# Two-layer attention and MLP step, forward and backward: a turn of w1, eight gradient products, small copies and the last output products change places

## The chip, the core and the metric

The kernel runs on one core of a Trainium2 chip. The metric is the device time of one execution in microseconds. The engines are PE (TensorE, matrix products; PEld are its weight loads), DVE (VectorE), ACT (ScalarE), POOL (GpSimd) and SP (SyncE, which here only issues loads). All loads are issued by SP, in one order; nearly all stores are issued by POOL.

## The reference

One decode step for two sequences (B = 2, one token each, width D = 1024) through attention A, MLP B, attention A, MLP B, with the same weights in both layers, and then the gradients of everything with respect to x, the caches and the weights.

```python
def _A_ref(x, k_cache, v_cache, wq, wo):          # 32 heads, 4 kv heads, 16384 cached keys, head size 128
    q = (x @ wq).reshape(B, Sq, Hq, Dh).transpose(0, 2, 1, 3)
    scores = einsum("bhqd,bhkd->bhqk", q, repeat(k_cache, 8)) * Dh ** -0.5
    o = einsum("bhqk,bhkd->bhqd", softmax(scores), repeat(v_cache, 8))
    return o.transpose(0, 2, 1, 3).reshape(B, Sq, Hq * Dh) @ wo

def _B_ref(x, w1, b1, w2, b2):                    # F = 3584
    h = gelu(einsum("bsd,df->bsf", layernorm(x), w1) + b1)
    return einsum("bsf,fd->bsd", h, w2) + b2

x = x + _A_ref(layernorm(x), ...)                 # layer 0
x = x + _B_ref(layernorm(x), ...)
x = x + _A_ref(layernorm(x), ...)                 # layer 1
x = x + _B_ref(layernorm(x), ...)
out, vjp = jax.vjp(f, x, k_cache, v_cache, wq, wo, w1, b1, w2, b2)
return (out, *vjp(grad_out))
```

Each cache has 2 x 4 x 16384 x 128 bf16 elements, 33.6 MB; its gradient is as large. The outputs are out_0 (x after both layers), out_1 (gradient of x), out_2 and out_3 (gradients of the K and V caches), out_4 to out_9 (gradients of wq, wo, w1, b1, w2, b2).

## The kernel before

**Passes.** The caches are read once for each of four passes: attention forward of layer 0 and of layer 1, then attention backward of layer 1 and of layer 0. A pass runs over 8 positions (one sequence and kv head each) of 16 steps; a step takes 8 rows of 128 keys. In a backward pass (`attn_bwd`) a step turns a block of V on DVE (L537), PE forms scores from it (L550), and 14 steps later K's products (`direct`, L575) collect the gradient of q in columns 0 to 7 of the PSUM tile sb0. At the end of a position `dq_of` copies these columns out, scaled (L1052), and sets them to zero (L1054). In the last pass (layer 0) the cache gradients are formed as well: `kv_outputs` turns blocks of probabilities and slopes (L1233) and multiplies them with the rows of q and of the output gradient (L1252); eight such products fill a 1 MB stage, which POOL stores (L1257).

**The order.** `Program.emit` collects pieces in a list, and `run` lays them out in this order, so that every engine's queue follows the list. Loads are handed out in the order of first use as slots come free (16 slots of 1 MB and some borrowed places). The order around the steps is written by hand: events at a step, background pieces (`bg`, released by a credit that rises with every step), `wb` for the weight products.

**The turn into the last pass.** At the end of the layer 1 backward pass the list is: `tail` (the last products with wq, L465), then the layer norm's backward (`attn_in_bwd`: `sums`, `rest`), which gives the gradient gA1 and its bf16 copy gM_all. Then w2 is multiplied with gM_all (`here_products`, L465, 28 times 8 products), which gives dh (L1504); dh is spread over quadrants (L506, L507) and multiplied with w1 (`turned_products`, L487, list `p1`, 8 times 28 products). For that, w1's eight loads of 896 KB are turned by DVE (`turn_rows`, L437, two turns for each load, list `t1`): two within the pass, two right after it, five among w2's products, seven after dh. The result is put back in order by `unquad` (L517 copies it out of PSUM; 16 small copies L525, L527, L529 on DVE, ACT and POOL go by the letters of `on`), and the MLP's layer norm backward (`mlp_in_bwd`, L649 on) gives gA_all (L929), which the first products of the last pass need (L465 again, with wo).

**Gradient products.** The gradients of the weights are outer products: `y_rows` (L1270) and `x_rows` (L1290) build rows, `dw_units` makes one product of 128 x 512 after the other (L1307), and ACT or DVE copies each out of PSUM (`cast_out`, L276, L279; the engine with the smaller estimated load takes it). Four of them fill a 512 KB stage, which POOL stores (L1333). `first` is the list for out_8 (w2): its first nine pieces stand between w1's products, six more between the MLP norm's two halves; `rest_h`, what is left of it, opens the background list.

**The end.** After the last step `attn_bwd` emits `todo`: the events, K's last output products (`kv_units`), `rows`, `tail`, the gradient products of wq's last part (`units`, 16 of them), and `parts`: the norm's sums (with the sum over partitions on PE, L594), its rest, and the row of out_1 (`col_to_row`, L617, L618, L619).

Of the kernel before, what the change touches and what calls it, by code (L numbers as in the profile page):

```python
# [29 lines left out]
N_END = 133  # L30
# [27 lines left out]
class Program:  # L58
# [12 lines left out]
    def emit(self, fn, uses=()):  # L71
        i = len(self.ops)
        self.ops.append((fn, tuple(uses)))
        for c in uses:
            if c.first is None:
                c.first = i
            c.last = i
# [105 lines left out]
def kernel(  # L183
# [25 lines left out]
    V = nc.vector  # L209
# [5 lines left out]
    _, HKV, SK, DH = A_k_cache.shape  # L215
# [3 lines left out]
    R = HQ // HKV  # L219
# [10 lines left out]
    emit = P.emit  # L230
# [14 lines left out]
    sb = [psp.tile([128, 512], F32, name=f"sb{i}") for i in range(2)]  # L245

    def flat(t):
        return t.rearrange("p a b -> p (a b)")

    half = {(i, f): flat(scb[i][f][:]) for i in range(2) for f in range(2)}  # L250
# [31 lines left out]
    def dve(us):  # L282
        load_of("dve", us)
# [65 lines left out]
    dq_all = vec.tile([128, HQ, 4], BF16, name="dq_all")  # L349
# [9 lines left out]
    saved = {}  # L359
# [150 lines left out]

        return (lambda: hold["vb"]), fn

    def unquad(dst, src, on="vag"):

        C = src.shape[1]
        q = small.tile([128, 8, 4, 2], F32, name="uq", bufs=1)[:, 0:C]
        V.tensor_copy(out=q, in_=src)  # L517
        n = 0
        for a in range(4):
            for j in range(4):  # L520
                d, s_ = dst[32 * a:32 * a + 32, :, j], q[32 * j:32 * j + 32, :, a]
                e = on[n % len(on)]
                n += 1
                if e == "v":
                    V.tensor_copy(out=d, in_=s_)  # L525
                elif e == "a":
                    S.copy(out=d, in_=s_)  # L527
                else:
                    GP.tensor_copy(out=d, in_=s_)  # L529
# [40 lines left out]
    def direct(acc, c, i, x, fresh=True):  # L570

        xv = x[:].rearrange("p (c j h y) -> p c j h y", c=NCH, j=4, y=8)
        for t in range(8):
            n = (i % 4) * 8 + t
            PE.matmul(acc, lhsT=c.ap[:, n * 128:(n + 1) * 128], rhs=xv[:, i // 4, t // 2, :, 2 * (i % 4) + t % 2],  # L575
                      start=(fresh and i == 0 and t == 0), stop=(i == 15 and t == 7),
                      skip_group_check=not fresh)
# [14 lines left out]
    def part_sum(src, n, at=None):  # L592
        ps = (ob() if at is None else at)[:, 0:n]
        PE.matmul(ps, lhsT=onesf, rhs=src, start=True, stop=True)  # L594
        return ps
# [48 lines left out]
        V.tensor_tensor(out=y[:], in0=xc[:], in1=bcast_j(rstd[:], DJ), op=ALU.mult)  # L644
        return y, rstd

    def ln_bwd_sums(dy, y, at=None):
        t1 = wrk.tile([128, DJ, 2], F32, name="lb_t1")
        V.tensor_tensor(out=t1[:], in0=dy, in1=y, op=ALU.mult)  # L649
        s = small.tile([128, 2, 2], F32, name="lb_s")  # L650
        V.tensor_reduce(out=s[:, 0, :], in_=dy.rearrange("p j b -> p b j"), axis=AX.X, op=ALU.add)
        V.tensor_reduce(out=s[:, 1, :], in_=t1[:].rearrange("p j b -> p b j"), axis=AX.X, op=ALU.add)
        return part_sum(flat(s[:]), 4, at)

    def ln_bwd_rest(ps, dy, y, rstd, twice=False):
        nm = small.tile([128, 2, 2], F32, name="lb_nm")
# [280 lines left out]
    vec_y, vec_r = {}, {}  # L937
# [83 lines left out]
                               lambda r: dq_all[:, k * R + r, 2 * l:2 * l + 2], l == 0) for j in range(DJ)]  # L1021
        return turns, prods

    def attn_bwd(l, order, gT, wo_first, outputs=None, mark=None, extra=None):

        kvs = []
        for g in order:
# [6 lines left out]
        ev, wb = {}, {}  # L1034
# [14 lines left out]

        def dq_of(pos, g):  # L1050
            def fn():
                V.tensor_scalar(out=dq_all[:, (g % HKV) * R:(g % HKV + 1) * R, 2 * l + g // HKV], in0=sb[0][:, 0:8],  # L1052
                                scalar1=QSCALE, scalar2=None, op0=ALU.mult)
                V.memset(sb[0][:, 0:8], 0.0)  # L1054
                dve(0.3)
            return fn

        xt = {}
# [8 lines left out]
        for pos, g in enumerate(order):  # L1067
            quick = l == 0 and pos == G - 1
            for f in range(2):
                n = 117 + 5 * f if quick else 16 * pos + 10 + 8 * f  # L1070
# [9 lines left out]
        tail = []  # L1080
        for i, k in enumerate(kvs):
# [16 lines left out]
            else:  # L1098
                if l == 0:
                    wb.setdefault(32 * i + 12 + LAG_B, []).append((dn_kept, ()))  # L1100
                ops, tail = wq_last_ops(l, k)
# [10 lines left out]
        s = 0  # L1112
        while s <= n_steps:
            if s in (10, 74) and mark is not None:
                mark(s // 64)
            pre = list(ev.pop(s, ()))
            fill = list(outputs(s)) if outputs is not None else []
            mids = []
            for v in k_at.get(s, ()):
                vpos, vi = divmod(v, 16)  # L1120
                vg = order[vpos]
                if vi % 4 == 0:
                    vc[0] = ld_kv("K", vg, vi // 4)
                c = vc[0]

                def pk(vpos=vpos, vg=vg, vi=vi, c=c):
                    direct(sb[0][:, 0:8], c, vi, xt[vpos % 2], False)

                mids.append((pk, [c]))
            n = -(-len(fill) // 3)  # L1130
            for fn, us in pre:
                emit(fn, us)
            between = fill[:n] + mids + fill[n:2 * n]
            for v in v_at.get(s, ()):
                pos, i = divmod(v, 16)
                if i % 4 == 0:
                    kc[0] = ld_kv("V", order[pos], i // 4)
                kblock(kc[0], i, scb[0], order[pos], between)
                between = []
            for fn, us in between:  # L1140
                emit(fn, us)
            if s not in v_at and pend:
                emit(*pend.pop(0))
            for fn, us in wb.pop(s, []) + (extra or {}).pop(s, []) + fill[2 * n:]:
                emit(fn, us)
            if l == 0 and s == 122:
                emit(lambda: obanks.extend([half[0, 0], half[0, 1]]))
            s += 1
        aflush()
        parts = attn_in_bwd(l, gT, dnq)  # L1150
        if l == 1:
            todo = tail + parts
        else:
            rows, kv_units, units = outputs(s, True)
            todo = ev.pop(s) + kv_units[0:2] + rows + tail[0:4] + kv_units[2:4] + tail[4:] + units[0:2] + parts[0:1]
            todo += units[2:5] + parts[1:2] + units[5:9] + parts[2:] + kv_units[4:] + units[9:]
        for b in todo:
            emit(*b)
        assert not ev and not wb and not pend and not extra, (ev, wb, extra)
# [1 line left out]
    def attn_in_bwd(l, gT, dnq):  # L1161
        h = {}

        def sums():
            dn = wrk.tile([128, DJ, 2], F32, name="dn")
            last = sb[0][:, 112:128].rearrange("p (j b) -> p j b", b=2)
            if l == 1:
                V.tensor_copy(out=dn[:], in_=last)
            else:
                V.tensor_tensor(out=dn[:], in0=last, in1=dnq[:], op=ALU.add)  # L1170
            h["dn"] = dn
            h["ps"] = ln_bwd_sums(dn[:], vec_y[f"a{l}"][:], half[0, 0] if l == 1 else sb[0][:, 200:])
            dve(0.8)

        def rest():
            dx = ln_bwd_rest(h["ps"], h["dn"][:], vec_y[f"a{l}"][:], vec_r[f"a{l}"][:])
            gn = saved[f"gA{l}"]
            V.tensor_tensor(out=gn[:], in0=dx[:], in1=gT()[:], op=ALU.add)
            dve(1.3)
            if l == 1:  # L1180
                V.tensor_copy(out=gM_all[:, :, 0:2], in_=gn[:])

        res = [(sums, ()), (rest, ())]
        if l == 0:
            res.append(col_to_row(saved["gA0"], out_1.rearrange("b s d -> (b s) d"), nc.sync))
        return res


    def kv_outputs(pos, g):

        res = []
# [28 lines left out]
        for c, w in [(c, w) for c in range(NCH) for w in (1, 0)]:  # L1220
            at_ = base + 4 * c + 4 * (pos == 0) if w == 1 else base + 14 + 4 * c
            if w == 0 and pos == G - 1:
                at_ = (124, 127, N_END + 1, N_END + 3)[c]
            stg = P.chunk(kind="full")
            hold = {}

# [17 lines left out]
                    dve(0.4)  # L1244
                hold["blk"] = blk

            res.append((at_ - 2, turn, ()))
            for u in range(8):
                def unit(c=c, w=w, u=u, hold=hold, stg=stg):
                    ps = ob()  # L1250
# [125 lines left out]
    up = [b * HKV + k for k in range(HKV) for b in range(2)]  # L1376
# [3 lines left out]
    def mark(name):  # L1380
        def f(n=0):
            marks[name, n] = len(P.ops)
        return f
# [56 lines left out]
    ws_o, wo_turns1, wo_prods = wo_first_ops(1, up[0] % HKV)  # L1440
# [27 lines left out]
    extra = {2: [(lambda: V.memset(fps1, 0.0), ())]}  # L1468
# [18 lines left out]
    for n, b in enumerate(t1[0:2]):  # L1487
        extra.setdefault(135 + 2 * n, []).append(b)
    extra[30] = [col_to_row(xM1, out_0.rearrange("b s d -> (b s) d"), kind="load")]
    attn_bwd(1, up, lambda: saved["g3"], (None, wo_prods), mark=mark("d1"), extra=extra)  # L1490
    wo_prods0 = wo_first_ops(0, down[0] % HKV, saved["wo"])[2]


    g2 = saved["gA1"]
    for b in t1[2:4]:
        emit(*b)
    for j in range(FJ):
        emit(*here_products(ws2c[j // 4], (j % 4) * 1024, 8, lambda j=j: dhps0[:, j, :],
# [14 lines left out]
        emit(*b)  # L1513
    emit(lambda: load_of("dve", 6.0))
    first = [y_rows(gM_all, 0, 8, 0, 0)] + dw_units("h", 0, 0, pieces_rows(out_8, F, D))
    rest_h = first[15:]
    for n, b in enumerate(p1):
        emit(*b)
        for u in first[n + (n > 0):n + 2]:
            emit(*u)  # L1520
    va0, spread_a0 = spread(lambda: gA_all[:, :, 0:2], DJ, "va")
    g1p = mlp_in_bwd(0, lambda dm: unquad(dm[:].rearrange("p (c j) b -> p c j b", j=4), dm_0), g2, parts=True)
    emit(g1p[0])
    emit(lambda: load_of("dve", 6.0))
    for u in first[9:15]:
        emit(*u)
    emit(lambda: saved.__setitem__("g1", g1p[1]()))
    extra = {4: [(spread_a0, ())]}
# [91 lines left out]
```

## Time and profile before

| | |
|---|---|
| median of 3 runs | 1110.19 us (1109.47 to 1112.6) |
| the profiled execution | 1110.15 us; span of its instructions 1108.4 us |
| PE, DVE, ACT, POOL busy | 815.9, 761.3, 493.1, 182.6 us |
| DMA | 450.03 MB, mean 406 GB/s |
| mean granted PE clock | 0.82 |
| last pass | about 671 to 1100 us |

The span runs from the first to the last instruction; busy times are sums over an engine's instructions, and the idle time of an engine counts only where others wait for it. In rows of stages the columns are: stretch, its length, busy time and count of each engine, the clock granted to PE, the DMA's busy share and its rate. In rows in order of time: start, length, engine, line, operation, tiles and shapes, and in brackets the idle time before it with what ended it.

### The profile page before, as it was taken

How to read it: one execution, taken by the hardware profiler on the slowest of the kernel's cores; microseconds unless marked ns; L12 is line 12 of the kernel's file. 1: busy time of each engine (PE TensorE's matmuls, PEld its weight loads, DVE VectorE, ACT ScalarE, POOL GpSimd, SP SyncE). 2: the span in 40 equal slices, each digit the busy share in tenths (PEclk: the TensorE clock that was granted, in tenths of full speed). 3: DMA queues.
4: the chain of work that ended last, by engine and by line, in shares of the span. 5: the costliest groups of instructions: out<-in, count | busy, mean ns of one | idle time of the engine just before them, and what ended most of it. 6: DMA issues, size and time to landing. Idle time of an engine off the chain costs nothing. (4 is left out here: it accounts for less than half of the span.)

```text
span 1108.4 us, 34192 instructions
## 1 busy us (share of the span) xinstructions
PE 815.9 (74%) x14689; PEld 609.3 (55%) x14689; DVE 761.3 (69%) x1474; ACT 493.1 (44%) x1133; POOL 182.6 (16%) x577
## 2 busy tenths in 40 slices
PE   5665666456888647888778678878876896698895
PEld 4554555455777547777677564444443443344453
DVE  5864665169888627665546476979776895598984
ACT  0322222102233222235434326767665785487874
POOL 1000000001000000111111101423332332233431
PEclk9999999997555555569868657999897998699998
DMA  9999999999999998999999989999999999999996
GB/s 372 421 422 421 422 425 421 398 404 399 418 423 421 422 421 345 409 419 421 419 423 416 417 318 411 355 399 422 420 420 425 423 419 422 420 402 421 410 423 250
DMA packets 97448, 450.03 MB, mean 406 GB/s; under 512 B 7528, under 2 KB 11638, under 8 KB 58512
## 3 DMA queue, kind: packets, MB, share of 16 engines
q1 hardware_dynamic: 79504, 349.22, 77.3%
q0 software_dynamic: 17792, 98.62, 21.6%
q8 instruction: 115, 1.88, 0.6%
q14 instruction: 37, 0.30, 0.1%
HBM read 349.20 MB, written 98.62 MB: 404 GB/s over the span
## 5 line engine op out<-in xcount | busy, mean ns | idle before, releaser
L537 DVE STREAM_TRANSPOSE kT<-slot 128x512 int32<-128x512 int32 x420 | 283.1, 694 | 112.8 <-PE sc L550 90.2
L550 PE MATMUL sc<-qbd,kT 128*128 128x32 bf16 x4096 | 262.5, 222 | 12.6 <-DVE kT L537 11.0
L550 PEld LDWEIGHTS <-kT 128*128 128x128 bf16 x4096 | 209.1, 115 | 64.7 <-issue 32.9
L575 PEld LDWEIGHTS <-slot 128*128 128x128 bf16 x3520 | 143.9, 103 | 106.7 <-issue 47.1
L575 PE MATMUL sb<-xt,slot 128*128 128x8 bf16 x3520 | 161.1, 176 | 49.0 <-DMA slot<-in_A_v_cache_dram 22.9
L276 ACT CAST slot<-sc 128x512 bf16<-128x512 f32 x293 | 167.0, 592 | 60.4 <-PE sc L1307 38.0
L1252 PE MATMUL sc<-slot,late 128*128 128x512 bf16 x350 | 131.1, 397 | 17.7 <-DVE slot L279 5.7
L279 DVE CAST slot<-sc 128x512 bf16<-128x512 f32 x171 | 114.3, 677 | 27.5 <-PE sc L1252 14.2
L760 ACT ACTIVATE e<-sc 128x512 bf16<-128x512 f32 x32 | 19.0, 597 | 235.9 <-DVE sc L757 169.0
L276 ACT CAST slot<-sb 128x512 bf16<-128x512 f32 x139 | 82.4, 593 | 37.1 <-PE sb L1307 17.0
L455 ACT COPY slot<-tp 128x512 int32<-128x512 int32 x88 | 50.3, 587 | 103.7 <-PE tp L452 103.4
L452 PE MATMUL tp<-ident,slot 128*128 128x128 bf16 x768 | 71.3, 255 | 13.2 <-ACT slot L455 6.0
L1252 PEld LDWEIGHTS <-late 128*128 128x128 bf16 x512 | 44.7, 98 | 62.2 <-issue 48.7
L585 ACT COPY xt<-e 32x128 int32<-32x128 int32 x256 | 75.6, 295 | 3.9
L1252 PE MATMUL sb<-slot,late 128*128 128x512 bf16 x162 | 65.6, 405 | 12.6 <-DVE slot L279 7.7
L1307 PE MATMUL sc<-slot,late 128*128 128x512 bf16 x159 | 64.0, 424 | 11.3 <-DVE e L279 6.2
L437 DVE STREAM_TRANSPOSE slot<-slot 128x1024 int32<-128x1024 int32 (+1 forms) x48 | 55.2, 1176 | 17.0 <-DMA slot<-in_A_wo_dram 8.0
L452 PEld LDWEIGHTS <-slot 128*128 128x128 bf16 x768 | 58.0, 116 | 15.9 <-issue 6.8
L279 DVE CAST slot<-sb 128x512 bf16<-128x512 f32 x81 | 54.9, 678 | 9.7 <-PE sb L1307 4.3
L642 POOL TENSOR_TENSOR m_rstd<-ln_vpe,neghalf 128x2 f32<-128x2 f32 x2 | 1.4, 715 | 349.6 <-DVE ln_vpe L640 349.6
L585 POOL COPY xt<-late 32x64 int32<-32x64 int32 x240 | 55.2, 230 | 13.0 <-DVE late L1046 1.9
L585 POOL COPY xt<-ds 32x64 int32<-32x64 int32 x128 | 29.5, 231 | 159.6 <-DVE ds L1046 104.7
(303 smaller groups left out, 1104.4 us busy)
## 6 DMA issues: line engine op xcount, KB each, us to landing
slot<-in_A_k_cache_dram SPq DMA_DIRECT2D x105, 1024.0 KB, 17.3
slot<-in_A_v_cache_dram SPq DMA_DIRECT2D x98, 1024.0 KB, 17.9
out_dram<-slot POOLq DMA_DIRECT2D x57, 1024.0 KB, 14.6
slot<-in_A_wq_dram SPq DMA_DIRECT2D x25, 1024.0 KB, 16.7
slot<-in_A_wo_dram SPq DMA_DIRECT2D x25, 1024.0 KB, 19.7
out_dram<-slot POOLq DMA_DIRECT2D x43, 512.0 KB, 13.9
slot<-in_B_w_dram SPq DMA_DIRECT2D x23, 896.0 KB, 15.4
slot<-in_B_w_dram SPq DMA_DIRECT2D x12, 1024.0 KB, 13.2
```

The lines of the kernel that those rows point to most:

```text
L276: S.copy(out=dst, in_=src)
L279: V.tensor_copy(out=dst, in_=src)
L437: V.transpose(out=t.ap[:, h * nw * 256:(h + 1) * nw * 256].bitcast(I32).rearrange("p (w j m) -> p w j m", j=4, m=32), in_=c.ap[:, 0:4 * nc ...
L452: PE.transpose(tp[:, j * 128:(j + 1) * 128], c.ap[:, off + j * 128:off + (j + 1) * 128], ident[:])
L455: S.copy(out=d.bitcast(I32), in_=tp.bitcast(I32))
L537: V.transpose(out=kT[:].bitcast(I32).rearrange("p (w j m) -> p w j m", w=4, j=4), in_=c.ap[:, (i % 4) * 1024:(i % 4 + 1) * 1024].bitcast(I ...
L550: PE.matmul(sc[:, a0:a0 + 4, :, 2 * (i % 4) + q], lhsT=kv[:, 2 * q + w, :, e], rhs=qbd[:, q_at(g), 2 * w + e], start=(w == 0 and e == 0), ...
L575: PE.matmul(acc, lhsT=c.ap[:, n * 128:(n + 1) * 128], rhs=xv[:, i // 4, t // 2, :, 2 * (i % 4) + t % 2], start=(fresh and i == 0 and t == ...
L585: (GP.tensor_copy if on[t % len(on)] == "g" else S.copy)(out=d[32 * t:32 * t + 32, c0:c0 + cn, j, :], in_=s[32 * j:32 * j + 32, c0:c0 + cn ...
L760: S.activation(out=e_of(l, g)[:, 8 * f:8 * f + 8].rearrange("p a h b -> p h a b"), in_=sc[f][:].rearrange("p h (a b) -> p h a b", b=8), fu ...
L1252: PE.matmul(ps, lhsT=hold["blk"][:, j, :], rhs=flat(qm(w)[:, (u % 2) * 4:(u % 2) * 4 + 4, :]), start=True, stop=True)
L1307: PE.matmul(ps, lhsT=hold[j // 4 * 4][:, j % 4, :], rhs=Y.ap[:, y_at + c0:y_at + c0 + cn], start=True, stop=True)
```

## The change

Six edits. (1) `unquad` shares its 16 copies by "vgvagvvg" instead of "vag". (2) At the end of the layer 1 pass the third turn of w1 (`t1[2]`) stands between `tail` and the norm instead of behind the norm. (3) In w1's phase only a `y_rows` and an `x_rows` stand between the products, four gradient products follow the sums, and `rest_h` begins at the seventh piece of `first`. (4) The K products of odd positions collect in columns 8 to 15 of sb0. (5) The norm's sums are split: what DVE does, and the sum over partitions on PE as a part of its own (`close`). (6) At the end K's last turn comes before the last step's products, and `todo` is put in another order. The order of loads on SP is the same in both kernels.

```diff
-    def unquad(dst, src, on="vag"):
+    def unquad(dst, src, on="vgvagvvg"):
...
-    def ln_bwd_sums(dy, y, at=None):
+    def ln_bwd_terms(dy, y):
...
-        return part_sum(flat(s[:]), 4, at)
+        return flat(s[:])
+
+    def ln_bwd_sums(dy, y, at=None):
+        return part_sum(ln_bwd_terms(dy, y), 4, at)
...
-    def attn_bwd(l, order, gT, wo_first, outputs=None, mark=None, extra=None):
+    def attn_bwd(l, order, gT, wo_first, outputs=None, mark=None, extra=None, mid=()):
...
-                V.tensor_scalar(out=dq_all[...], in0=sb[0][:, 0:8],
+                acc = sb[0][:, pos % 2 * 8:pos % 2 * 8 + 8]
+                V.tensor_scalar(out=dq_all[...], in0=acc,
                                 scalar1=QSCALE, scalar2=None, op0=ALU.mult)
-                V.memset(sb[0][:, 0:8], 0.0)
+                V.memset(acc, 0.0)
...
-                    direct(sb[0][:, 0:8], c, vi, xt[vpos % 2], False)
+                    direct(sb[0][:, vpos % 2 * 8:vpos % 2 * 8 + 8], c, vi, xt[vpos % 2], False)
...
         if l == 1:
-            todo = tail + parts
+            todo = tail + list(mid) + parts
         else:
             rows, kv_units, units = outputs(s, True)
-            todo = ev.pop(s) + kv_units[0:2] + rows + tail[0:4] + kv_units[2:4] + tail[4:] + units[0:2] + parts[0:1]
-            todo += units[2:5] + parts[1:2] + units[5:9] + parts[2:] + kv_units[4:] + units[9:]
+            todo = ev.pop(s) + kv_units[0:4] + rows + kv_units[4:6] + tail[0:4] + kv_units[6:8] + tail[4:] + kv_units[8:10]
+            todo += parts[0:1] + units[0:4] + parts[1:2] + units[4:8] + parts[2:3] + kv_units[10:13] + parts[3:]
+            todo += kv_units[13:] + units[8:]
...
-            h["ps"] = ln_bwd_sums(dn[:], vec_y[f"a{l}"][:], half[0, 0] if l == 1 else sb[0][:, 200:])
+            h["s"] = ln_bwd_terms(dn[:], vec_y[f"a{l}"][:])
             dve(0.8)
+
+        def close():
+            h["ps"] = part_sum(h["s"], 4, half[0, 0] if l == 1 else sb[0][:, 200:])
...
-        res = [(sums, ()), (rest, ())]
+        res = [(sums, ()), (close, ()), (rest, ())]
...
-                at_ = (124, 127, N_END + 1, N_END + 3)[c]
+                at_ = (124, 127, N_END + 1, N_END + 2)[c]
...
-            res.append((at_ - 2, turn, ()))
+            res.append((min(at_ - 2, N_END - 1), turn, ()))
...
-    attn_bwd(1, up, lambda: saved["g3"], (None, wo_prods), mark=mark("d1"), extra=extra)
+    attn_bwd(1, up, lambda: saved["g3"], (None, wo_prods), mark=mark("d1"), extra=extra, mid=t1[2:3])
...
-    for b in t1[2:4]:
+    for b in t1[3:4]:
         emit(*b)
...
-    rest_h = first[15:]
+    rest_h = first[6:]
     for n, b in enumerate(p1):
         emit(*b)
-        for u in first[n + (n > 0):n + 2]:
-            emit(*u)
+        if n in (3, 5):
+            emit(*first[n // 4])
...
-    for u in first[9:15]:
+    for u in first[2:6]:
         emit(*u)
```

More of the change, by code (lines that the diff above doesn't have):

```diff
@@ L1051, in fn @@
             def fn():
-                V.tensor_scalar(out=dq_all[:, (g % HKV) * R:(g % HKV + 1) * R, 2 * l + g // HKV], in0=sb[0][:, 0:8],
+                acc = sb[0][:, pos % 2 * 8:pos % 2 * 8 + 8]
+                V.tensor_scalar(out=dq_all[:, (g % HKV) * R:(g % HKV + 1) * R, 2 * l + g // HKV], in0=acc,
                                 scalar1=QSCALE, scalar2=None, op0=ALU.mult)
-                V.memset(sb[0][:, 0:8], 0.0)
+                V.memset(acc, 0.0)
                 dve(0.3)
```

## The prediction

> **What bounds the kernel now.** I read the page's DMA rows first: 450 MB at a mean of 406 GB/s, with most slices near 421. At 421 GB/s the bytes alone take 1069 us of the 1108.4 us span. So a change can win only where the DMA stands still or thin, unless it lets an engine catch up that is last. The busy time by stage shows where that is (after the engines come clock, DMA share and GB/s).
>
> ```profile
> 646.00:660.00 14.00, 11.41 (x335) 10.42 (x335) 13.46 (x15) 3.79 (x5) 0.00 (x0) 0.50 0.93 346
> 660.00:664.00 4.00, 4.00 (x111) 3.17 (x109) 2.25 (x3) 2.24 (x4) 0.81 (x2) 0.50 0.25 59
> 692.00:726.00 34.00, 30.30 (x346) 16.07 (x346) 30.95 (x50) 25.96 (x49) 13.51 (x43) 1.00 0.94 350
> 726.00:913.00 187.00, 154.37 (x1806) 81.06 (x1806) 151.01 (x263) 132.63 (x263) 61.33 (x183) 0.93 1.02 421
> 945.00:1086.00 141.00, 120.05 (x1498) 66.82 (x1498) 114.80 (x198) 102.98 (x207) 49.70 (x145) 0.93 1.01 415
> 1086.00:1092.00 6.00, 4.94 (x34) 2.13 (x31) 3.51 (x14) 3.56 (x7) 0.72 (x1) 0.72 0.21 85
> ```
>
> The turn (646 to 664) and the end (1086 to 1092) are thin. From 692 to 726 PE and DVE are about 90% busy and the rate is 350: the engines pace the start of the last pass, and no engine's wait there is on a DMA. From 726 the DMA is full. The chain of waits has one long piece on a load, and none after it:
>
> ```profile
> 913.34 31.38 DMA e<-in_A_v_cache_dram
> ```
>
> So loads pace the pass up to 945; after it engine work is last, with the DMA as full. Next the turn's instructions in order of time (start, length):
>
> ```profile
> 646.00 7.22 DVE L437 STREAM_TRANSPOSE slot<-slot 128x896 int32<-128x896 int32 x7
> 653.15 0.18 DVE L1504 SCALAR_TENSOR_TENSOR dh_all<-sb,nslope 128x56 bf16<-128x56 f32 x1
> 654.77 7.52 DVE L437 STREAM_TRANSPOSE slot<-slot 128x896 int32<-128x896 int32 x7
> 662.32 0.80 SPq L373 DMA_DIRECT2D slot<-in_A_v_cache_dram  x2
> 665.38 0.17 DVE L517 COPY uq<-sb 128x16 f32<-128x16 f32 x1 [3.09 <-PE sb L487]
> 667.53 0.17 DVE L649 TENSOR_TENSOR lb_t<-dm_sb,m_y 128x16 f32<-128x16 f32 x1 [0.90 <-ACT dm_sb L527]
> 670.04 0.17 DVE L929 CAST gA_all<-gM 128x16 bf16<-128x16 f32 x1
> 671.03 1.12 PE L465 MATMUL sb<-gA_all,slot 128*128 128x2 bf16 x36
> ```
>
> **The change, part by part** (against the profiled run: 1108.4 us span, 1110.15 us, 0.04 below the median, so I use its times as they are).
>
> One turn ahead of the norm. The seven turns from 646.00 end at 653.2; PE's products for the same step end at 652.24, so the turns hold L1504 back by 0.9. With six (6 x 1.03) they end at 652.2 and L1504 starts at 652.3: 0.85 saved. The moved turn stands in front of the norm's first copy, L1168 at 643.39, and waits for w1's second load; the landings in the trace put that at 642.34, after the K load whose landing PE waits for at 640.06. 642.34 + 1.03 = 643.37: covered with 0.02 to spare; if the load lands x later, the norm, w2's products behind it and the rest of the turn are x later. I take 0.05. The V load at 662.32 is released by the last turn, so it gains only these 0.85.
>
> Gradient products out of w1's phase. Six of them and three row builds stand between w1's products (L487) and make PE wait for casts; L517 comes at 665.38. Without them L507 ends at 654.0; 224 products at 0.03 each are 6.6, y_rows 0.94, x_rows 0.34: PE ends at 661.9, the seven later turns end at 661.45 and 28 products (0.93) behind them at 662.4. So L517 starts at 662.4: 2.95 earlier, the 0.85 included.
>
> Copies shared otherwise. 16 small copies: DVE 6, ACT 5, POOL 5 become 8, 2, 6. Here ACT's started late behind casts, so L649 came 2.15 after L517. Afterwards DVE needs 8 x 0.173 = 1.39 and POOL 6 x 0.219 = 1.31: 1.63 after L517, 0.5 saved. At 438 ACT was not late, and L649 goes from 1.44 to 1.65 after L517: 0.2 lost, under loads that follow; I take 0. In the three other uses DVE's L994 waits for POOL, whose one more copy costs 0.2; two are before 945 under a full DMA, the third (L994 at 961.61, after waiting 2.48) counts: +0.2.
>
> ```profile
> 438.46 1.06 DVE L525 COPY dm_sb<-uq 32x4 f32<-32x4 f32 x6
> 438.56 1.09 POOL L529 COPY dm_sb<-uq 32x4 f32<-32x4 f32 x5 [22.60 <-DVE uq L517]
> ```
>
> These two run side by side, and POOL's 0.218 each is what dnq's sixteen copies take with nothing beside them (3.51/16). The Trainium skill ("SBUF — State Buffer", SBUF: two separate sides) says that a fp32 copy on VectorE and a GpSimd operation lock each other out for whole instructions; by it the shares would add up, not overlap. The rows do not show that; it is the fourth rival.
>
> Six gradient products behind the sums were on PE until L465 at 671.03, though gA_all was there at 670.2; four are done in time: 0.8 saved. Sum of the turn: 2.95 + 0.5 + 0.8 = 4.25, so the last pass's first products start near 666.8.
>
> What that costs later. In the order of the changed kernel 8 products, one row build and two 512 KB stores go into the background of the last pass, spread over some 115 steps of about 3.1 us. One product writes 131 KB and takes a cast of about 0.635 us on DVE or ACT, half of that with both at work. Up to 726 about 1.6 of them come (0.5 us). From 726 to 945 the DMA is full: 6.4 are still owed at 726 and 2.2 at 945, so 0.55 MB more must pass, 1.3 us at 421 GB/s. After 945 the last 2.2 cost 0.7 by either measure. Sum 2.5; its bounds are 0 (hidden in the engines' waits for loads, about 19 us between 740 and 945) and 5 (8 casts on one engine that is last). I take 2.5, because at a full DMA there is no free place for bytes.
>
> dq in two halves. The accumulator alternates between columns 0 to 7 and 8 to 15 of sb0, so the K products (L575) should no longer wait for the memset (L1054). That wait is 1.6 us in all, 1.1 of it at 1076.30. But both halves lie in one PSUM tile, and in the order of the changed kernel L575 still waits for DVE's memset at each position. I take 0; bounds 0 and -1.6. The Trainium skill ("PSUM — Partial Sum Buffer", PSUM bank collisions raise a hardware error) says to guard PSUM by bank and quadrant, not by address; by that rule too it is 0, against 1.6 saved by the edit's wording.
>
> The end. The last turn moves ahead of the last products, K's output products go before and between the dq products, the norm's sum gets four products ahead of it.
>
> ```profile
> 1087.92 0.46 PE L594 MATMUL sb<-lb_s,one 128*128 128x4 f32 x2 [1.06 <-DVE lb_s L652]
> 1089.89 0.15 DVE L657 TENSOR_SCALAR lb_nm<-sb 128x4 f32<-128x4 f32 x1
> 1092.04 0.68 DVE L618 CAST slot<-sc 2x512 bf16<-2x512 f32 x1 [0.35 <-ACT slot L276]
> 1099.59 0.74 POOL L1333 DMA_DIRECT2D out_dram<-ds  x1 [0.48 <-issue]
> ```
>
> From 1092.04 on 19 casts and the row's copies keep DVE and ACT full for 7.0 us (19 x 0.635 + 1.34 + 0.4, halved). In the changed order 11 casts are left there: 4.2 to 4.5. But three casts stand ahead of the norm's scaling on DVE, and PE has 8 more transposes and four more products ahead of it, so I put the row's copies 1.7 later. Difference 0.8 to 1.1. The other bound: all casts and copies from 1083.4, evenly shared, need 12.6 us and end at 1096.0, 3.0 earlier than 1099.03. The worst: PE stands idle before the row's transposes, its clock falls to half as in 1086 to 1092 (0.72 there), and the 11 products take 0.43 each: 0.5 later. I take -1.6, because the 1.06 of idle PE ahead of L594 is filled as well. The last store's way (issue to landing 6.2) stays.
>
> Sum: -4.25 + 0.05 + 2.5 + 0.2 - 1.6 = -3.1, so 1107.0 us.
>
> **The rivals.** First, the payback is hidden: background products fall into the engines' waits, and only 0.5 + 0.2 come back: -4.25 + 0.7 - 1.6, about 1105.0. For it: PE and DVE are near 80% busy from 726 to 913. Against: DMA share 1.02.
>
> Second, slower: loads pace the last pass from the turn on. Place: the V load at 662.32, 0.85 earlier only. The DMA idled at 660 to 664, where work was cheap, and 1.05 MB goes to full stretches: +2.5; 0.2 for POOL; and a pass that reaches the end on late loads gains nothing from casts that come sooner, while PE's added transposes ahead of the last products cost up to 0.5. -0.85 + 2.5 + 0.2 = +1.85, about 1112; with a half clock at the end and the bounds of the payback up to 1114. For: 664 to 692 runs at 408 GB/s. Against: no engine waits for a DMA from 670 to 740. It decides if L437 or L537 waits for loads before 726.
>
> Third, the turn does not do what it says: w1's second load comes a microsecond later, the norm waits, and the end's two effects cancel: 1109 to 1110.5, no change.
>
> Fourth, the lock: 1.3 more for 8 + 6 copies in turn, at five places; if all count, 1107.0 + 6.5 = 1113.5.
>
> **How the numbers follow.** 0.3%, 3.3 us, is about what a measurement of this kernel can tell from no change: faster is below 1106.9, slower above 1113.5. Forecast 0.45 (its own range 1105 to 1109, half of it faster, half the same), first rival 0.20 (faster), second 0.25 (0.15 slower, 0.10 the same), third and fourth 0.05 each. Faster 0.43, same 0.37, slower 0.20. For 8 in 10 the range leaves out the lower half of the first rival and the upper part of the second and fourth: 1103 to 1113.
>
> **What would show it.** Right: L1504 near 652.3, L517 near 662.4, the first L465 of the last pass near 667, the long wait for a V load ending near 942.5, the last store issued near 1096.5. Wrong: L1168 later than 643.6; L465 early but the same V load landing at 945 (second rival); L525 and L529 one after the other (fourth); L575 of a position starting before the memset of the one before it (the halves of dq work after all, 1.6 more). The forecast falls if the stretch 726 to 945 is shorter by itself, or the end's last store later than that V load's gain.

## The result, and the profile after

The changed kernel takes 1117.46 us (median of 6 runs, 1116.11 to 1119.99) against 1110.91 (1109.47 to 1112.6): ratio 1.0062, interval 1.0052 to 1.0072, so by the ratio 6.9 us slower, where 3.1 less was forecast. Its profiled execution took 1116.11 us, with a span of 1114.3. Some lines have new numbers in what follows: L1252 became L1260, L1285 became L1293, L1333 became L1341 (products of the cache gradients, clearing of the x rows, stores of the weight gradients); L1504 became L1512, L1168 became L1173.

The stages, columns as before:

```profile
646.00:660.00 14.00, 11.11 (x369) 10.71 (x369) 13.26 (x18) 2.31 (x2) 0.00 (x0) 0.50 0.90 333
660.00:664.00 4.00, 3.00 (x101) 2.91 (x98) 3.09 (x9) 1.33 (x4) 0.60 (x4) 0.50 0.45 125
692.00:726.00 34.00, 29.16 (x280) 14.15 (x280) 27.22 (x43) 23.37 (x44) 11.76 (x36) 0.90 0.76 292
726.00:913.00 187.00, 151.51 (x1785) 80.07 (x1783) 146.10 (x259) 127.68 (x249) 60.36 (x183) 0.92 1.01 417
1086.00:1092.00 6.00, 6.00 (x139) 4.80 (x136) 3.88 (x9) 2.77 (x6) 0.53 (x1) 1.00 0.98 408
```

The stretch 660 to 664 is less empty, as forecast. The last row says nothing of the end: the pass runs some 7 us later here (the last of the slopes, a step on DVE that comes twice in each position, starts at 1072.9, before at 1065.4), so 1086 to 1092 still lies in it, and the thin place comes at 1094 to 1096 (45 GB/s). From 726 on the DMA is nearly as full as before (417). But 692 to 726 fell from 350 to 292 GB/s, at a clock of 0.90 instead of 1.00. 58 GB/s over 34 us are 2.0 MB, and at the 0.42 MB per us of a full DMA that is 4.7 us. No term of the sum lay there but 0.5.

The turn, DVE and then POOL in order of time:

```profile
643.20 1.11 DVE L437 STREAM_TRANSPOSE slot<-slot 128x896 int32<-128x896 int32 x1 [1.51 <-PE sb L465]
644.23 0.14 DVE L1173 COPY dn<-sb 128x16 f32<-128x16 f32 x1
653.08 0.21 DVE L1512 SCALAR_TENSOR_TENSOR dh_all<-sb,nslope 128x56 bf16<-128x56 f32 x1
663.03 0.17 DVE L517 COPY uq<-sb 128x16 f32<-128x16 f32 x1 [0.78 <-PE sb L487]
663.24 1.38 DVE L525 COPY dm_sb<-uq 32x4 f32<-32x4 f32 x8
664.75 0.18 DVE L649 TENSOR_TENSOR lb_t<-dm_sb,m_y 128x16 f32<-128x16 f32 x1
667.26 0.17 DVE L932 CAST gA_all<-gM 128x16 bf16<-128x16 f32 x1
```

```profile
663.27 1.32 POOL L529 COPY dm_sb<-uq 32x4 f32<-32x4 f32 x6 [20.04 <-DVE uq L517]
```

Everything up to the norm's output came earlier, as forecast, but in smaller steps: the MLP norm's result (L932) comes 24.7 us after the last group of products with wq begins (642.59 to 667.26), before 27.7 (642.36 to 670.04).

What happened at the start of the last pass, on DVE and on POOL:

```profile
694.01 0.69 DVE L279 CAST slot<-sb 128x512 bf16<-128x512 f32 x1 [0.27 <-issue]
698.00 0.69 DVE L279 CAST slot<-sc 128x512 bf16<-128x512 f32 x1 [3.30 <-DMA out_dram<-slot]
```

```profile
689.44 0.72 POOL L1341 DMA_DIRECT2D out_dram<-slot  x1 [0.21 <-ACT late L268]
690.21 4.34 POOL L585 COPY xt<-late 32x64 int32<-32x64 int32 x16
```

The cast at 698.00 waited 3.30 us for a store, not for PE: the store out of its stage was issued at 689.44 and landed at 697.90. In the order of the program this store and the cast that refills its stage are 79 instructions apart (all engines counted); the nearest such pair of before is 175 apart (the nearest refill, as it is called below). Four stages of 512 KB are open at this point, and two of them hold the rows of the queries for positions 0 and 1, so the gradient products go round in the other two. DVE works in order, so the turns of V behind the cast wait too, PE runs dry, and then this happens to its clock (the third number from the right, ahead of DMA share and rate):

```profile
697.00:698.00 1.00, 0.00 (x0) 0.00 (x0) 0.01 (x1) 0.00 (x0) 0.00 (x0) 1.00 0.98 401
699.00:700.00 1.00, 1.00 (x11) 0.52 (x10) 0.94 (x2) 0.21 (x1) 0.00 (x0) 0.50 0.00 0
704.00:705.00 1.00, 1.00 (x11) 0.38 (x9) 0.94 (x3) 0.97 (x2) 0.00 (x0) 0.50 0.94 393
706.00:707.00 1.00, 1.00 (x19) 0.61 (x18) 0.99 (x2) 0.78 (x2) 0.51 (x1) 1.00 0.65 156
```

PE is idle for some 3.2 us and then has half its clock for 6.8 us. Between the first and the second slope (L1043, after L1046) both kernels run the same 205 products and 33 DVE operations. Before took 21.3 us, after 26.7 (first line before, second after):

```profile
689.35:710.62 21.27, 19.27 (x205) 10.11 (x205) 19.12 (x33) 16.60 (x33) 7.51 (x22) 1.00 0.96 369
687.55:714.30 26.75, 22.15 (x205) 10.77 (x204) 20.11 (x33) 16.83 (x34) 7.60 (x23) 0.87 0.77 297
```

The second thing that is new is in the list of waits from 660 on (who waited for whom, us in total, times, longest). Before:

```profile
DVE late L271 <- POOL late L1285: 3.5, 2, 1.8
ACT late L268 <- POOL late L1285: 1.6, 1, 1.6
```

After:

```profile
PE sb L575 <- DVE sb L1058: 1.1, 1, 1.1
DVE late L271 <- POOL late L1293: 8.2, 3, 4.9
ACT late L268 <- POOL late L1293: 7.6, 3, 3.3
DVE slot L279 <- DMA out_dram<-slot: 6.3, 3, 3.3
```

The x rows are copied into a tile that POOL clears first, and this clearing now stands behind POOL's sixteen xt copies (L585, 4.3 us): 15.8 us of waits on ACT and DVE instead of 5.1. (The first and the last line are used further down.)

A ledger helps to place the loss: bytes of all DMA packets that had ended by a time, less those of before, in MB (positive is ahead). The kernels are introduced below. It is one trace of each; what stands at 692 has come up earlier.

```
by                       692    726    800    840   1000   1050   1086
after                  -0.12  -2.11  -2.25  -3.04  -2.37  -2.67  -2.73
e1, products out       -0.14  -2.28  -2.78  -4.52  -3.81  -4.01  -4.06
e4, one product less   +0.15  +0.09  -0.02  -1.69  -1.02  -1.73  -1.71
g4, both waits gone    -0.37  -0.41  -0.45  -1.21  -0.56  -0.27  -0.53
e2, products back      -0.24  -0.06  -0.05  -0.03  +0.11  -0.04  -0.06
```

2.73 MB at 1086 are 6.5 us, about the whole loss.

### The profile page after: what moved, and what is told of

Its sections match the earlier page's. It is cut to its first block, busy times and chain, and to the rows that moved or that the text cites. A ratio compares the mean times of both kernels' runs of the same rounds, so it can differ in the third digit from the quotient of the medians.

```text
span 1114.3 us, 34201 instructions
## 1 busy us (share of the span) xinstructions
PE 814.0 (73%) x14689; PEld 608.1 (55%) x14689; DVE 765.0 (69%) x1488; ACT 488.1 (44%) x1114; POOL 183.6 (16%) x582
## 3 DMA queue, kind: packets, MB, share of 16 engines
q0 software_dynamic: 17792, 98.62, 21.3%
## 5 line engine op out<-in xcount | busy, mean ns | idle before, releaser
L575 PEld LDWEIGHTS <-slot 128*128 128x128 bf16 x3520 | 144.0, 103 | 108.5 <-issue 47.2
L575 PE MATMUL sb<-xt,slot 128*128 128x8 bf16 x3520 | 161.0, 177 | 49.0 <-DMA slot<-in_A_v_cache_dram 24.1
L276 ACT CAST slot<-sc 128x512 bf16<-128x512 f32 x274 | 156.5, 594 | 40.8 <-PE sc L1315 19.6
L1260 PE MATMUL sc<-slot,late 128*128 128x512 bf16 x336 | 126.9, 401 | 29.9 <-DVE slot L279 9.6
L279 DVE CAST slot<-sc 128x512 bf16<-128x512 f32 x182 | 121.4, 676 | 32.9 <-PE sc L1315 12.2
L276 ACT CAST slot<-sb 128x512 bf16<-128x512 f32 x154 | 91.2, 592 | 45.4 <-PE sb L1315 22.5
L1260 PEld LDWEIGHTS <-late 128*128 128x128 bf16 x512 | 45.1, 99 | 64.3 <-issue 51.1
L585 ACT COPY xt<-e 32x128 int32<-32x128 int32 x256 | 75.6, 295 | 3.9
L1260 PE MATMUL sb<-slot,late 128*128 128x512 bf16 x176 | 70.4, 400 | 7.8 <-DVE slot L279 3.8
L1315 PE MATMUL sc<-slot,late 128*128 128x512 bf16 x172 | 64.5, 400 | 7.9 <-DVE slot L279 4.0
L585 POOL COPY xt<-late 32x64 int32<-32x64 int32 x240 | 55.2, 230 | 14.9 <-DVE late L1049 4.2
L279 DVE CAST slot<-sb 128x512 bf16<-128x512 f32 x70 | 47.5, 679 | 12.1 <-PE sb L1260 6.4
L585 POOL COPY xt<-ds 32x64 int32<-32x64 int32 x128 | 29.5, 231 | 158.4 <-DVE ds L1049 116.1
```

The lines of the kernel that those rows point to most:

```text
L276: S.copy(out=dst, in_=src)
L279: V.tensor_copy(out=dst, in_=src)
L585: (GP.tensor_copy if on[t % len(on)] == "g" else S.copy)(out=d[32 * t:32 * t + 32, c0:c0 + cn, j, :], in_=s[32 * j:32 * j + 32, c0:c0 + cn ...
L1260: PE.matmul(ps, lhsT=hold["blk"][:, j, :], rhs=flat(qm(w)[:, (u % 2) * 4:(u % 2) * 4 + 4, :]), start=True, stop=True)
L1315: PE.matmul(ps, lhsT=hold[j // 4 * 4][:, j % 4, :], rhs=Y.ap[:, y_at + c0:y_at + c0 + cn], start=True, stop=True)
```

## The experiments

All ratios are to before, run on the same chip; 0.001 is 1.1 us.

**Which edit.** Three kernels split the change.

e1 is before with edit 3 alone:

```diff
-        for u in first[n + (n > 0):n + 2]:
-            emit(*u)
+        if n in (3, 5):
+            emit(*first[n // 4])
...
-    for u in first[9:15]:   ...   rest_h = first[15:]
+    for u in first[2:6]:    ...   rest_h = first[6:]
```

> Before with only the gradient products taken out of w1's phase (8 products and two stores go to the last pass). Theory A, the stage wait: in the program order a DVE cast refills stage 1b 79 instructions after the store out of it was issued (nearest such distance before: 175), DVE stands still for some 3 to 4 us near 694, PE runs dry, its clock falls to about 0.57 for some 8 us, and the first stretch of the pass loses 5.5 us; with 2.5 us for the deferred bytes and some 2.5 us gained at the turn the kernel takes about 1116. Theory B, the bytes alone: no such wait is needed, the 8 products cost their casts and bytes at a full DMA, +2.5 less the turn's gain: 1110 to 1112. Theory C, the end or the dq halves are at fault: at most 1109, as the turn's gain is kept and nothing at the end is changed.

Measured: 1119.99, ratio 1.0072 (1.0060 to 1.0085). Edit 3 alone costs as much as the whole change, or a little more, and 4 us more than theory A gave it. The DVE wait for a store is there (3.4 us).

e2 is the changed kernel with exactly this hunk undone.

> The changed kernel with the gradient products put back into w1's phase; all other edits kept. Theory A: the nearest refill of a stage is 175 instructions behind its store again, no DVE wait on a store before 726, granted clock 1.0 from 689 to 714, and the time falls to 1107 to 1109. Theory B: 1114 to 1116 (the 2.5 us of deferred bytes saved, some of the turn's gain lost). Theory C: 1115 or more, as what costs the time is still in.

Measured: 1111.17, ratio 0.9996 (0.9988 to 1.0005). No wait for a store up to 726. Theories B and C expected 1114 and more, and theory A, with 1107 to 1109, expected too much: the other five edits together are worth nothing that can be measured.

e3 is before with edits 5 and 6 (the end) alone.

> Before with only the order of the end changed (last turn, K's output products, the norm's sum in two steps). Prediction's term: -1.6, so about 1109.3; the trace of the changed kernel hints at less, -0.7: 1110.2. Theory C, the end costs time: above 1112.

Measured: 1111.05, ratio 0.9998 (0.9989 to 1.0007). The end's -1.6 did not come, and it cost nothing either: theory C falls.

**The wait for a stage.** e4 takes one product away from the front of the pass, which shifts the stages against the rows of the queries:

```diff
-    rest_h = first[6:]      ...   for u in first[2:6]:
+    rest_h = first[5:]      ...   for u in first[2:5]:
```

> The changed kernel with one gradient product fewer ahead of the last pass (five units of the first list instead of six, the sixth goes to the background): one product more is deferred, and the phase of the stages against the query stages shifts, so that the nearest refill is 207 instructions behind its store instead of 79. Theory A: the wait of 3 to 4 us and the low clock behind it go, 1112 to 1114. Theory B: 0.3 us slower than the changed kernel, about 1117.8.

Measured: 1113.76, ratio 1.0023 (1.0014 to 1.0031). Putting off one product more makes it 4.3 us faster. f4 makes the same edit to e1:

> Before with only the gradient products out of w1's phase, but five units ahead of the pass instead of six, so that the nearest refill lies 207 instructions behind its store and not 79. Theory A: the wait of 3 to 4 us and the low clock go, 1115 to 1116 against 1120.0 with the wait. Theory B: 1120.3.

Measured: 1113.86, ratio 1.0023 (1.0015 to 1.0032), 5.4 us below e1, somewhat more than expected. In neither is there a wait for a store up to 726, and the stretch 692 to 726 is back at 346 GB/s and full clock in e4 (first line; the second is used below):

```profile
692.00:726.00 34.00, 30.68 (x370) 16.81 (x370) 30.63 (x49) 26.71 (x49) 11.94 (x34) 1.00 0.94 346
1000.00:1035.00 35.00, 26.04 (x264) 13.17 (x265) 24.56 (x42) 21.20 (x39) 10.47 (x27) 0.90 1.01 419
```

f1 and f2 try the reverse, a wait planted into before by starting the background later:

```diff
-        if s >= 5:
+        if s >= 7:        # f1; f2: s >= 8
```

> Before with the background of the last pass starting at step 7 instead of 5 and nothing else changed: some 3 units come later, and in the program order an ACT cast refills a stage 82 instructions after its store is issued. Theory A (the wait for a stage is what costs): slower than before by 1.5 to 4, so 1112.5 to 1115, and slower than its neighbour that starts at step 8. Theory B (what counts is how much is put off): 0.5 to 1 above before, and a little faster than the neighbour.

> Before with the background starting at step 8: one more step put off than its neighbour, but the nearest refill of a stage lies 155 instructions behind its store. Theory A: no wait for a store before 726, 1111 to 1112, faster than the neighbour. Theory B: 1112 to 1113, slower than the neighbour.

Measured: f1 1120.20, ratio 1.0086 (1.0071 to 1.0101); f2 1116.61, ratio 1.0052 (1.0038 to 1.0065). f1 has the planted wait, on ACT:

```profile
699.81 0.59 ACT L276 CAST slot<-sb 128x512 bf16<-128x512 f32 x1 [3.35 <-DMA out_dram<-slot]
```

Theory A was right that the wait comes in f1 and not in f2, and that f1 is the slower; both its times were too small. f1 needs 25.6 us from the first to the second slope (before 21.3), but also 33.6 from the 13th to the 14th (before 29.4), and f2, without a wait for a store, 33.8 there. f2's list of waits from 880 to 1045 shows two long ones on POOL, the second of them in this stretch:

```profile
DVE late L271 <- POOL late L1285: 5.0, 1, 5.0
ACT late L268 <- POOL late L1285: 4.8, 1, 4.8
```

**The clearing of the x rows.** So a second collision moves with the background. (That it makes f2's loss is read from these rows; no run takes it out of f2.) In e4 it is plainest near 1014, on POOL and then on ACT:

```profile
1009.37 4.29 POOL L585 COPY xt<-late 32x64 int32<-32x64 int32 x16
1013.61 0.57 POOL L1265 DMA_DIRECT2D out_dram<-slot  x1
1014.22 0.52 POOL L1293 MEMSET late<- 128x512 bf16 x1
```

```profile
1014.77 0.36 ACT L268 COPY late<-sc 4x256 int32<-4x256 int32 x1 [4.47 <-POOL late L1293]
```

The 16 copies, a store, the clearing, and only then ACT's copy, after 4.47 us. PE is idle from 1011 to 1015 and at half clock until 1021.6, 6.8 us again. Between the 13th and the 14th slope e4 needs 34.8 us, before 29.4 for as many products and casts. The g kernels clear the rows on DVE:

```diff
-                GP.memset(Xt[b][:], 0.0)
+                V.memset(Xt[b][:], 0.0)
```

g1 is e4 with it, g2 the changed kernel, g3 before, g4 is g1 with the old shares of edit 1.

> The changed kernel with five units ahead of the pass (no stage wait) and the clearing of the x rows (128x512 memset, one per change of rows) on DVE instead of POOL. Theory M: the shift of the background put three of POOL's memsets behind the sixteen xt copies (4.3 us) in POOL's queue, near 791, 901 and 1014; ACT or DVE waits 4 to 5.6 us there and PE falls to half clock; without that the copies of the x rows wait under 1 us, the stretch between the 13th and 14th slope takes 29.5 us instead of 34.8, and the time falls from 1113.8 to 1109 to 1110, at or a little below before. Theory D (the debt in bytes): nothing of it is touched, 1113.5 to 1114.

> The changed kernel as it is, stage wait kept, with only the memset on DVE. Theory M: what the stage wait leaves after the loads have caught up near 950 is 3.7 us, the rest of the loss (4.3 us, 1008 to 1042) goes: 1113 to 1114. Theory D: 1117.5.

> Control: before with only the memset on DVE. Its waits for POOL's memset are 5.1 us in all, none over 1.8: theory M expects 1110 to 1111, theory D 1111.

> The run with five units and the memset on DVE, with the small copies shared as before the change (DVE 6, ACT 5, POOL 5). With the products out of w1's phase ACT is no longer late, and the trace of the run with only the products out has the norm 1.38 us behind L517 against 1.72 with the new shares: 0.3 earlier at the turn, so 0 to 0.5 faster than with the new shares.

Measured: g1 1112.41, ratio 1.0013 (1.0005 to 1.0022); g2 1117.14, 1.0057 (1.0044 to 1.0071); g3 1115.50, 1.0042 (1.0030 to 1.0055); g4 1111.67, 1.0008 (0.9999 to 1.0017). The stretch answered: 28.9 us from the 13th to the 14th slope in g1 and g4, and PE's clock stays full there (g4):

```profile
1000.00:1035.00 35.00, 30.05 (x350) 15.85 (x349) 31.66 (x53) 27.38 (x52) 10.72 (x27) 1.00 1.02 421
```

But g1 gained only 1.1 us of the 4 expected, g2 next to nothing (theory M had 1113 to 1114), and the control lost 4.7. The control's reason is at the turn, where the first clearing is DVE's too:

```profile
655.70 7.52 DVE L437 STREAM_TRANSPOSE slot<-slot 128x896 int32<-128x896 int32 x7
663.23 0.55 DVE L1285 MEMSET late<- 128x256 uint32 x2
671.25 0.17 DVE L517 COPY uq<-sb 128x16 f32<-128x16 f32 x1 [7.47 <-PE sb L487]
```

It stands behind seven turns, and the x rows, the products and L517 wait for it (671.25, before 665.38). The h kernels therefore leave the first one on POOL (`(GP if xn == "h" else V).memset`): h1 is before with this, h3 is e2, and h4 is e4 with the old shares.

> Fair control: before with the memset of the x rows on DVE from the second gradient on (the first one, at the turn, stays on POOL). Theory M: before's waits for the memset are 5.1 us in all, none over 1.8, most of them in stretches where loads pace the pass: 1110 to 1111. If the memset on DVE costs by itself: 1112 or more.

> All edits but the products (they stay in w1's phase), memset on DVE within the pass: neither stage wait, nor debt, nor long waits for POOL. If turn and end give what their rows say (0.7 at the turn, 2.7 at the last store's issue): 1108 to 1110, below before. If the slowest of the sixteen DMA engines ends the program whatever is issued earlier: 1110.5 to 1111.5.

> Five units ahead of the pass, old shares, memset on DVE within the pass, all work done. Compared with the run of the same name without the pass condition the first memset is back on POOL: 1110.5 to 1112. Theory M, with a debt of nine products: turn -3.0, debt +2.8, so 1111.

Measured: h1 1111.41, ratio 1.0000 (0.9992 to 1.0009); h3 1110.34, 0.9996 (0.9987 to 1.0005); h4 1112.14, 1.0004 (0.9995 to 1.0012). h1 shows that moving the clearing is worth nothing in before. h4 has the changed turn and the products put off, without the two collisions, and is level with before. From the changed kernel to h4 it is 6.4 us: 4.3 for the stage (e4), 2.1 for the clearing and the shares. In the 2.1 the steps are 1.1 (g1), 0.6 (g4) and 0.4 (h4); none of them alone is clear of noise, only their sum. What the clearing does by itself is shown in the stretch (34.8 to 28.9 us), not in the time.

Why is an earlier turn only level? For one thing it is less early in h4: in its profiled execution L932 comes 25.9 us after the last group with wq began, 1.8 less than in before, as PE stands idle for 2.03 us ahead of the row build at L1278 for no reason that the profile shows. And in g4 the last slope (1062.6) is 2.8 us ahead of before, yet the last packet (1106.6) is 1.4 behind: the engines are early and the bytes are not. The waits of DVE and ACT for stores in g4 from 660 on, where before has none:

```profile
DVE slot L279 <- DMA out_dram<-slot: 7.3, 5, 1.9
ACT slot L276 <- DMA out_dram<-slot: 4.6, 4, 2.0
DVE e L279 <- DMA out_dram<-e: 3.6, 1, 3.6
ACT e L276 <- DMA out_dram<-e: 1.8, 1, 1.8
```

The two for e are at the end of the pass (1080), the others between 694 and 1072; h4 has the like, none before 726. Such waits need not show in the time: e2 has one too (2.3 us at 799) and is level with before. The changed kernel's at 698 lies where the engines pace the pass.

**The debt.** What could hold the bytes back is the price of the products that were put off. f3 and h2 meant to take it away by not doing eight of them: f3 is e4, h2 is h4 with `rest_h = first[5:6] + first[7:8] + first[15:]`.

> The changed kernel with five units of the first list ahead of the pass (no stage wait, as in the run with one product less), and the eight products and two stores that the edit put off are not done at all: rows 256 to 767 of the first gradient of the MLP are left out. The rest of the background then comes where it came before the change. It prices the debt: by the prediction's term of 2.5, 1111.3; by the bytes missing at equal times in the run with one product less (1.7 MB between 800 and 840, 4 us), 1109.8; if the debt is hidden in waits for loads, 1113.8 as with them.

> Five units ahead of the pass, old shares, memset on DVE within the pass, and the eight products and two stores that the edit put off not done at all (rows 256 to 767 of the first gradient are left out). Debt theory: 2.5 us (1.05 MB at 0.42 MB per us) below the same kernel with them: 1109 if that one is at 1111.5. If the debt costs nothing: the same as that one.

Measured: f3 1114.59 (1111.31 to 1117.81 over 12 runs), ratio 1.0025 (1.0014 to 1.0037); h2 1111.17, 1.0007 (0.9997 to 1.0017). Neither gained, and neither settles it. With the eight out, an x row comes right behind the first product of the pass, and the engines stall around it: ACT's copy of the row waits 1.17 us for the clearing, and a DVE copy 3.27 for ACT. h2 from 680 on:

```profile
680.00:684.00 4.00, 1.46 (x22) 1.20 (x22) 0.71 (x1) 2.12 (x6) 1.41 (x3) 0.73 1.01 334
684.00:688.00 4.00, 4.00 (x27) 2.02 (x26) 3.07 (x5) 2.23 (x5) 0.00 (x0) 0.50 0.99 365
```

Its first slope is at 689.6, 22.3 us after L932; in e4 and before that way takes 19.4. The fix leaves every instruction in place but two stores near 770, where the DMA is full: k1 is before, k2 is h4 with

```diff
             def store(ap, j0=j0, rb=rb, cb=cb, cn=cn):
+                if out_ap is out_8 and j0 >= 24:
+                    return
```

> Before with the last two stores of the first gradient left out (rows 3072 to 3583; the products and casts are still done): 1.05 MB less near 770, where the DMA is full. If bytes set the end: 2.5 us less, 1108.5. If loads that wait for engines, or the tail of the end, set it: 1110 to 1111.

> The same two stores left out of the kernel with five units ahead, old shares and the memset on DVE within the pass (1112.1), whose background is nine products behind that of before. If bytes set the end: 1109.6, and the debt has the price that the prediction gave it (2.5). If not: 1112, and the debt is not what takes the turn's gain.

Measured: k1 1108.33, ratio 0.9976 (0.9966 to 0.9986); k2 1108.32, 0.9975 (0.9965 to 0.9985). 1.05 MB in the full stretch cost 2.7 us in before and 3.2 in h4. As a price of bytes the 2.5 stands.

No kernel that writes all the outputs is faster than before by more than can be measured; h3, the best, is level with it.

## Why the prediction was wrong, point by point

**One turn ahead of the norm** (0.85). L1512 came 10.5 us after the last group with wq began (642.59 to 653.08), before 10.8: 0.3. The term that was mis-sized is the +0.05: the moved turn began at 643.20 and the norm at 644.23, 0.65 after PE was done with that group. The sign set for the third rival (the norm later than 643.6) came, but not by the load: w1's second load landed at 642.51, 0.08 before that group began (in before 0.09: at 642.27, where the prediction read 642.34). The turn's row names what it waited for, PE's products with wq, for 1.51 us, and every kernel with edit 2 has the same wait (1.51 or 1.52). The prediction looked only at the landing; why the turn has to wait for these products was not tested.

**Products out of w1's phase** (2.1 of the 2.95). L517 came 9.95 us after L1512, before 12.23: 2.3. Right.

**Copies shared otherwise** (0.5). In e2 L649 comes 1.72 after L517, before 2.15: 0.4. But in e1, with the old shares and the products out, 1.38: ACT was late only because of the products that edit 3 takes away, so behind edit 3 the new shares lose 0.34. Two gains were added that remove the same wait: this 0.5 is another term that failed. The fourth rival falls: eight copies on DVE take 1.38 and six on POOL 1.32, side by side, so the lock that the Trainium skill ("SBUF — State Buffer", SBUF: two separate sides) describes is again not in these rows.

**Fewer products behind the sums** (0.8). L465 began 0.23 after L932, before 0.99: 0.8, as forecast. With it the pass's first products are 3.8 early against the last group with wq (4.2 forecast), but it does not last: in e4 the first slope comes 19.4 us after L932, as in before.

**What it costs later** (+2.5). As a price of bytes this was right: 2.7 and 3.2 in k1 and k2 for the same 1.05 MB. But it was the only cost looked for, and this is the step that failed: "8 products, one row build and two 512 KB stores go into the background". Not only these move: the whole background behind them, some 190 pieces, shifts against the fixed work of the steps. In before it met the stages' landings and POOL's queue where they hardly collided, and that was luck; shifted, they meet a stage whose store is under way (4.3 us) and a clearing behind sixteen copies (2.1 with the shares). Of the 10 us between the forecast and the result, 6.4 are these two collisions, for which the sum had no term. f2, a mere shift, loses 5.8 with the same pieces of work.

**dq in two halves** (0). L575 still waits for the memset, 1.1 us at the one long place as before. Right; the rule of the Trainium skill ("PSUM — Partial Sum Buffer", PSUM bank collisions raise a hardware error) to guard by bank and quadrant gives the same.

**The end** (-1.6). The last store is issued earlier, in e2 2.7 us (1096.86 against 1099.59):

```profile
1096.86 0.72 POOL L1341 DMA_DIRECT2D out_dram<-ds  x1 [0.49 <-issue]
```

The thin stretch itself was filled: 1086 to 1092 carries 315 GB/s at full clock in e2, where before had 85 and 0.72. The time did not follow. The stretches behind the last store, e2 first and then before:

```profile
1097.00:1101.00 4.00, 0.00 (x0) 0.00 (x0) 0.00 (x0) 0.00 (x0) 0.59 (x1) 0.67 0.90 365
1101.00:1103.00 2.00, 0.00 (x0) 0.00 (x0) 0.00 (x0) 0.00 (x0) 0.00 (x0) 0.50 0.06 27
1103.00:1106.00 3.00, 0.00 (x0) 0.00 (x0) 0.00 (x0) 0.00 (x0) 0.00 (x0) 0.50 0.04 18
```

```profile
1097.00:1101.00 4.00, 1.26 (x6) 0.29 (x3) 2.03 (x4) 1.94 (x4) 2.01 (x3) 1.00 0.97 397
1101.00:1103.00 2.00, 0.00 (x0) 0.00 (x0) 0.00 (x0) 0.00 (x0) 0.00 (x0) 0.69 0.97 391
1103.00:1106.00 3.00, 0.00 (x0) 0.00 (x0) 0.00 (x0) 0.00 (x0) 0.00 (x0) 0.50 0.45 184
```

Nearly all of e2's bytes are through by 1101, but 18 to 27 GB/s go on to 1105.2, where before ends as well. That is about one DMA engine's rate of the sixteen (421/16 = 26). "The last store's way (issue to landing 6.2) stays" was the error: from issue to last packet it is 5.7 us in before and 8.3 in e2.

**The second rival** (slower) gave 1.85, as loads pace the pass. In part it was so: six kernels (e4, f3, f4, g1, g4, h2) have their tenth slope 5 to 10 us behind before and their eleventh between 950.3 and 951.1, ahead of its 951.9. What collides ahead of that point is partly won back there, what collides behind it is not. The chain of waits has lost its long V load: after's longest piece is a store that a cast waits for, 7.90 us at 1037.75.

Sum as measured: stage +4.3, clearing and shares +2.1, and +0.4 (-0.6 to 1.3) for what h4 has left, the earlier turn and the debt together: 6.8 of the 6.9, the end and the halves being nothing (e2, e3). No run parts the turn from the debt. The rows give the turn 3.0 in the changed kernel and 1.8 in h4, k1 and k2 put the debt near 2.9; with either the two come close to cancelling.

## What to carry to other kernels

Where work is taken out of one place and put into a list that feeds idle places, look at everything behind it in that list: for each buffer that goes round, how many instructions lie between the store out of it and the next write into it, and for each helper on a shared in-order queue, what now stands ahead of it. The order of the changed program shows both before any run; here the nearest refill fell from 175 to 79 instructions, while f2, with 155, had no wait of this kind and was 5.8 us slower all the same. And two gains that end the same wait are one gain.

## What the runs showed of the hardware

PE was idle for about 3.2 us (from 695.5) in the changed kernel and 4.2 us (from 1011) in e4, and each time the granted clock was 0.50 for 6.8 us from then on, though PE was busy nearly all along. So a wait of 3.3 us cost 5.4. The Trainium skill ("TensorE: Matmul & The Clock Gate", Part 1) says that an idle window of about 3.4 us throttles the array; the first trace comes close to it. It also says that about 3.4 us of sustained work release it; here it took twice that. Elsewhere in the last pass of these two traces, and of before, a stretch at 0.50 that began there lasted 3.4, 6.8 or 10.2 us, apart from the one at the end (in before 3.4 us from 743.3, behind 3.3 of idle time).

In the last pass one of a store's sixteen landings falls behind the others: the last comes less than 0.2 us after the one before it up to 730, 5.7 us from 1020 to 1050 and about 7 up to 1095 (medians over stores and loads of the profiled run before). A stage is free, and the program over, only with the last of them. Which engine it is and why was not found.
